# Gate logits of a mixture of experts: x as the stationary operand, and seven operations in a round of the normalisation in place of eight

## The chip, the cores and the metric

The kernel runs on one core of a Trainium2 chip. The metric is the device time of one execution in microseconds. The core's engines are named as in the profile: PE (TensorE, matmuls; PEld is its weight load), DVE (VectorE), ACT (ScalarE), POOL (GpSimd), SP (SyncE, which issues most DMAs).

## The reference

Attention in a window of 64, an ELU MLP on 2304 tokens of width 512, and then a mixture of 8 experts whose gates are normalised over rows and columns in turn. The change touches only how `logits` and `P` are computed.

```python
def _moe2_ref(x, w_gate, w1, w2):
    N, D = x.shape                      # 2304, 512
    E = w_gate.shape[1]                 # 8
    logits = x @ w_gate
    logits = logits - logits.max()
    P = np.exp(logits)
    for _ in range(8):
        P /= P.sum(1, keepdims=True) + 1e-09
        P /= P.sum(0, keepdims=True) + 1e-09
        P *= N / E
    out = np.zeros((N, D), dtype=np.float32)
    for e in range(E):
        h = np.maximum(x @ w1[e], 0.0)
        ye = h @ w2[e]
        out += P[:, e:e + 1] * ye
    return out
```

## The kernel before

The 2304 tokens lie in five blocks j of 512, 512, 512, 512 and 256 tokens. Every operand of a large matmul is split into a high part rounded to fp32r and a low part (the rest), and a product takes three fp32r matmuls. x of block j is held as `Xh[j]` and `Xl[j]`, features on the partitions, tokens along the free dimension, four chunks c of 128 features.

The order on every engine is that in which the code is written. The MLP runs in steps (u, j, i): u is one of four groups of 512 hidden features, i one of its four chunks. A step issues `step_in` (12 matmuls into a bank `p1`, then the ELU on ACT and DVE), and then `step_out` of the step two before it: 12 matmuls into four banks `ac` that stay open over i. At i = 3 DVE adds the four banks to `acc` (L493, `accs_done`), which frees them; there are four such banks, so `step_out` at i = 0 of the next block waits for these adds. The experts' stage follows in the same way: steps e0, e1, ... with `e_in` (12 matmuls, then `relu`: ACT writes `hh`, DVE writes `hl`) and `e_out` of two steps before (12 matmuls into four banks for the 512 tokens of block 0, 6 into two banks for the 256 tokens of block 1 that this stage takes). e0 and e1 are the two chunks of block 0 for the first unit of weights, e2 and e3 the same of block 1, and e4 opens the second unit, whose first `e_out` stands in e6; the `e_out` in e4 is that of e2 and opens block 1's two banks. When a unit's last chunk of a block is done, the banks are copied or added to `acc` (`e_done`: on ACT, L897, for the first unit).

Beside these steps a list `extra` is worked off. In the last group u = 3, when a block has its x complete, `moe1_out` appends for it: store x and split chunks 0 and 1, split chunks 2 and 3, nothing, `gate_a`, `gate_b`. One entry is taken at the end of a step of the MLP, up to two at the end of an experts' step while gates are left, and a step ends at a `gate_a`. `x2_split` makes the high part on ACT (L497) and leaves the low part on DVE (L501) to the next step. `gate_a` computes the logits of the block with the gate weights `gw` as the stationary operand (16 of its 128 columns are in use: the 8 high and the 8 low parts) and x as the moving one, 512 columns at a time; the result has 16 partitions. DVE copies it to `lgT`, and `gate_b` turns it with `sel`, a 16x8 matrix that also adds the two parts, so that a token comes to lie on a partition; the 8 logits of each token are copied to `Lg`. Behind the last block stand the entries of the normalisation (`sink_parts`): the maximum, the exponential, and eight rounds `rows` and `cols`, one entry a round.

When no gate is left in `extra`, the pool `big1` (x of blocks 2 to 4, `gw`) is closed and the pool B, which overlays it, is opened (`done2`). This lets through the tasks that prepare the experts' weights, `p_tasks`: for half an expert n, POOL makes four sums into `sw` (two buffers, L704), ACT writes the high parts of `rw` and `sw` (L729), DVE the low parts (L734), SP stores them. The tasks are let through by a table `due` against `clock`, the sum of 256-token units that the steps have done, and before `done2` only up to the 58th.

Of the kernel before, what the change touches and what calls it, by code (L numbers as in the profile page):

```python
# [8 lines left out]
F32 = mybir.dt.float32  # L9
# [3 lines left out]
ALU = mybir.AluOpType  # L13
AX = mybir.AxisListType
# [4 lines left out]
def kernel(  # L19
# [14 lines left out]
    nc = tc.nc  # L34
    B, H, S, D = q.shape
    NT, DM = out.shape
    DFF = w_in.shape[1]
    E, _, FF = w1.shape
    P = 128
    WIN = 64  # L40
    NCC = DM // P
# [5 lines left out]
    TB = 512  # L47
    scale = 1.0 / float(D) ** 0.5
    blocks = [(t, min(TB, NT - t)) for t in range(0, NT, TB)]
    NTT = NT // P  # L50

    def r(ap):
        return ap.bitcast(F32)

    const = ctx.enter_context(tc.tile_pool(name="const", bufs=1))
    def pool(name, side="left", **kw):
        cm = tc.tile_pool(name=name, bufs=1, side=side, reuse_waits="tile", **kw)
        return cm, cm.__enter__()
# [3 lines left out]


    mask = const.tile([P, P], F32, name="mask")
    sel = const.tile([2 * E, E], F32, name="sel")
    gwr = const.tile([P, NCC, E], F32, name="gwr")
    pad_cm, pad = pool("pad", side="right")
    ctx.callback(close, pad_cm)
# [4 lines left out]
    work_cm, work = pool("work")  # L73
# [9 lines left out]
    ident = const.tile([P, P], F32, name="ident")  # L83
    ones = const.tile([P, P], F32, name="ones")
    Lg = const.tile([P, NTT, E], F32, name="Lg")
# [3 lines left out]
    Xh = [home[j].tile([P, NCC, n], R32, name=f"xh{j}") for j, (_, n) in enumerate(blocks)]  # L89
    Xl = [home[j].tile([P, NCC, n], R32, name=f"xl{j}") for j, (_, n) in enumerate(blocks)]  # L90
# [12 lines left out]
    gw = big1.tile([P, NCC, P], R32, name="gw")  # L103
# [7 lines left out]
    def ps_sm(name):  # L111
        return ps.tile([P, 512], F32, tag="sm", bufs=1, name=name)
# [428 lines left out]
    def moe1_out(st, extra):  # L541
        step_out(st)
        u, j, i = st
        if u == NU - 1 and i == UF - 1:
            fs = [
                lambda: (x2_store(j), x2_split(j, (0, 1))), lambda: x2_split(j, (2, 3)),
                lambda: None, lambda: gate_a(j), lambda: gate_b(j),
            ]
            logits.append(fs[3])
            gate_fs.extend(fs)  # L550
            extra += fs
            if j == len(blocks) - 1:
                extra += sink_parts()


    lgT = {}

    def gate_a(j):
        n = blocks[j][1]
        lg = ps_sm("lg")  # L560
        for c in range(NCC):
            nc.tensor.matmul(lg[:, :n], gw[:, c, :], Xh[j][:, c, :], start=(c == 0), stop=False)
            nc.tensor.matmul(
                lg[:, :n], gw[:, c, :], Xl[j][:, c, :], start=False, stop=(c == NCC - 1)
            )
        t = work.tile([P, TB], F32, tag="m", bufs=2, name="lgT")[:2 * E]
        nc.vector.tensor_copy(t[:, :n], lg[:2 * E, :n])
        lgT[j] = t

    def gate_b(j):  # L570
        t0, n = blocks[j]
        lt = ps_sm("lt")
        nt = n // P
        t = lgT.pop(j)
        for tt in range(nt):
            nc.tensor.matmul(
                lt[:, tt * E:(tt + 1) * E], t[:, tt * P:(tt + 1) * P], sel, start=True, stop=True
            )
        nc.vector.tensor_copy(
            Lg[:, t0 // P:t0 // P + nt, :], lt[:, :nt * E].rearrange("p (t e) -> p t e", e=E)  # L580
        )

    sk = {}
# [1 line left out]
    def sink_parts():  # L585
        def small(shape, nm):
            return const.tile(shape, F32, name=nm)

        def p0():
            mx = small([P, 1], "mx")  # L590
            nc.vector.tensor_reduce(mx, Lg, axis=AX.XY, op=ALU.max)
            sk["mx"] = mx

        def p1():
            t = ps_sm("mxT")
            nc.tensor.matmul(t[0:1, :P], sk["mx"], ident, start=True, stop=True)
            nb = small([1, 1], "nb")
            nc.vector.tensor_reduce(nb, t[0:1, :P], axis=AX.X, op=ALU.max, negate=True)
            sk["nb"] = nb

        def p2():
            t = ps_sm("nbB")
            nc.tensor.matmul(t[:, 0:1], ones[0:1, :], sk["nb"], start=True, stop=True)
            nm = small([P, 1], "nm")
            nc.vector.tensor_copy(nm, t[:, 0:1])
            nc.scalar.activation(Pr, Lg, AF.Exp, bias=nm)
            sk["rs"] = small([P, NTT], "rs")
            sk["cs"] = small([P, E], "cs")
            sk["rc"] = small([P, E], "rc")

        def rows():
            rs, cs = sk["rs"], sk["cs"]
            nc.vector.tensor_reduce(rs, Pr, axis=AX.X, op=ALU.add)
            nc.vector.tensor_scalar(rs, rs, 1e-9, None, op0=ALU.add)
            nc.vector.reciprocal(rs, rs)
            nc.vector.tensor_tensor(
                out=Pr, in0=Pr, in1=rs.unsqueeze(2).to_broadcast([P, NTT, E]), op=ALU.mult
            )
            nc.vector.tensor_reduce(cs, Pr.rearrange("p t e -> p e t"), axis=AX.X, op=ALU.add)

        def cols():
            t = ps_sm("csum")
            nc.tensor.matmul(t[:, :E], ones, sk["cs"], start=True, stop=True)
            rc = sk["rc"]
            nc.vector.tensor_scalar(rc, t[:, :E], 1e-9, None, op0=ALU.add)
            nc.vector.reciprocal(rc, rc)
            nc.vector.tensor_scalar(rc, rc, float(NT) / E, None, op0=ALU.mult)
            nc.vector.tensor_tensor(
                out=Pr, in0=Pr, in1=rc.unsqueeze(1).to_broadcast([P, NTT, E]), op=ALU.mult
            )  # L630

        def first():
            p2()
            rows()

        def mid():
            cols()
            rows()

        return [p0, p1, first] + [mid] * 7 + [cols]  # L640
# [267 lines left out]
    def x2_store(j):  # L908
        if j == 1:
            for o, a in ((0, acc[j]), (2, acc1b)):  # L910
                nc.sync.dma_start(out=x2d[j][:, o:o + 2], in_=a.rearrange("p (c t) -> p c t", c=2))
        else:
            nc.sync.dma_start(out=x2d[j], in_=acc[j].rearrange("p (c t) -> p c t", c=NCC))
# [240 lines left out]
    with tc.manual_schedule():  # L1154
# [6 lines left out]
            out=mask[:WIN], in_=mask[:WIN], compare_op=ALU.is_gt, fill=-1.0e9 / scale,  # L1161
# [4 lines left out]
            out=mask[:WIN], in_=mask[:WIN], compare_op=ALU.is_ge, fill=-1.0e9 / scale,  # L1166
# [51 lines left out]
        for m in range(NST + 3):  # L1218
# [57 lines left out]
        nc.gpsimd.tensor_tensor(  # L1276
            out=gw[:, :, E:2 * E], in0=gwr, in1=r(gw[:, :, 0:E]), op=ALU.subtract
        )
        nc.vector.tensor_copy(sel[0:E, :], ident[0:E, 0:E])
        nc.sync.dma_start(out=sel[E:2 * E, :], in_=ident[0:E, 0:E])  # L1280
        run_bg(len(bg))
        bg += [w_tasks(2 * UF + m)[1] for m in range(2)]
        for kk in range(2 * UF + 2, 4 * UF):
# [20 lines left out]
        for s, st in enumerate(steps):  # L1304
            u, j, i = st
# [9 lines left out]
            while len(queue) > 2:  # L1315
                moe1_out(queue.pop(0), extra)
# [39 lines left out]
        for u in range(1, 2 * KP):  # L1356
            n = 5 if 0 <= u - 2 < len(others) - N1 - N3 else 4
# [5 lines left out]
        for s, st in enumerate(esteps):  # L1363
            _, u, j, x = st
# [57 lines left out]
        for s in range(NPD * 7 + LAG):  # L1422
            k, j = divmod(s, 7)
# [61 lines left out]
```

## Time and profile before

| | |
|---|---|
| median of three runs | 2016.78 us (2015.24 to 2019.64) |
| the profiled execution | 2017.01 us, span 2015.0 us |
| PE busy | 1990.0 us, 99% of the span |
| DVE busy | 1410.5 us, 70% |
| ACT busy | 871.4 us, 43% |
| POOL busy | 754.3 us, 37% |
| DMA queue q1 | 479.24 MB, 74.1% of 16 engines |

The span is what the profiler saw of the program; the execution's own time is some 2 us longer. Busy means that an instruction of the engine was under way; matmuls are pipelined, so that a new one starts before the last has ended.

### The profile page before, as it was taken

The page shows a single profiled execution, that of the slowest core. Times are in us where ns is not written, and L with a number is a line of the kernel's source. Part 1 is how long each engine was busy: PE and PEld are TensorE (multiplying, and loading weights), DVE is VectorE, ACT ScalarE, POOL GpSimd, SP SyncE. Part 2 cuts the span into 40 slices and gives each one's busy share as a digit, 9 for nine tenths or more (in the row PEclk, how much of TensorE's full clock was granted, in tenths as well). Part 3 has the DMA queues.
Part 4 walks back from the last instruction along what each step waited for, and adds up shares of the span by engine and source line. Part 5 has one row for each costly group of instructions (what it writes and reads, how often), then busy time and mean ns, then how long its engine had stood idle before and what let it go on. Part 6 is the DMA issues. An engine that isn't in the chain of part 4 may idle for free.

```text
span 2015.0 us, 36376 instructions
## 1 busy us (share of the span) xinstructions
PE 1990.0 (99%) x13190; PEld 1845.5 (92%) x13190; DVE 1410.5 (70%) x2727; ACT 871.4 (43%) x1839; POOL 754.3 (37%) x725
## 2 busy tenths in 40 slices
PE   9999999999999999999999999999999999999998
PEld 7778888888878888889999999999999999999998
DVE  6745676757688666557777777777777777777776
ACT  8866455545444343333343333333334333333332
POOL 5423242323355555343253233333334323333332
PEclk9999999999999999999999999999999999999999
DMA  9741254438599999958878777777888878777774
GB/s 210 161 106 40 79 177 153 164 126 317 203 368 339 368 367 357 343 192 275 278 247 276 248 247 249 250 250 250 250 278 263 257 250 250 250 248 249 248 248 129
DMA packets 290866, 481.59 MB, mean 239 GB/s; under 512 B 78528, under 2 KB 145152, under 8 KB 286848
## 3 DMA queue, kind: packets, MB, share of 16 engines
q1 hardware_dynamic: 290608, 479.24, 74.1%
q8 instruction: 105, 1.72, 0.3%
q14 instruction: 73, 0.60, 0.1%
q10 hardware_dynamic: 80, 0.03, 0.0%
HBM read 348.14 MB, written 126.88 MB: 236 GB/s over the span
## 4 chain that ended last, share of the span: by engine, by line
PE 86%; DVE 5%; issue 3%; DMA 2%; ACT 2%; POOL 1%; SPq 1%; DVEq 0%; POOLq 0%; ACTq 0%
PE la L1051 15%; PE ob L1124 13%; PE oa L1124 13%; PE lb L1051 11%; PE ac L883 2%; PE ac L884 2%; PE ac L885 2%; PE p L865 2%; PE p L866 2%; PE p L867 2%; PE p L204 2%; PE p L205 2%; PE p L206 2%; PE ac L532 2%; PE ac L533 2%
## 5 line engine op out<-in xcount | busy, mean ns | idle before, releaser
L1033 POOL TENSOR_TENSOR h<-s,h 128x384 fp32r<-128x384 f32 x304 | 373.0, 1246 | 712.9 <-ACT h L1024 641.8
L1051 PE MATMUL la<-xf,w1f 128*128 128x384 f32 x1824 | 361.4, 336 | 6.9 <-ACT a L1064 4.8
L1051 PEld LDWEIGHTS la<-xf,w1f 128*128 128x128 f32 x1824 | 311.7, 189 | 9.1 <-ACT a L1064 5.2
L1124 PE MATMUL oa<-w2f,h 128*128 128x256 f32 x2394 | 307.3, 282 | 0.8 <-DVE acc L1145 0.8
L1124 PE MATMUL ob<-w2f,h 128*128 128x256 f32 x2394 | 307.2, 282 | 0.0
L1124 PEld LDWEIGHTS oa<-w2f,h 128*128 128x128 f32 x2394 | 302.0, 190 | 1.0 <-DVE acc L1145 1.0
L1124 PEld LDWEIGHTS ob<-w2f,h 128*128 128x128 f32 x2394 | 302.0, 190 | 0.0
L1029 DVE SCALAR_TENSOR_TENSOR h<-c,h 128x384 fp32r<-128x384 f32 x228 | 211.0, 925 | 120.9 <-ACT h L1024 120.7
L1051 PE MATMUL lb<-xf,w1f 128*128 128x384 f32 x1368 | 274.8, 335 | 0.0
L1051 PEld LDWEIGHTS lb<-xf,w1f 128*128 128x128 f32 x1368 | 237.7, 189 | 0.2 <-DVE c L1081 0.2
L1024 ACT ACTIVATE h<-s 128x384 fp32r<-128x384 f32 x304 | 154.8, 524 | 146.9 <-DVE s L1068 60.8
L1024 ACT ACTIVATE h<-c 128x384 fp32r<-128x384 f32 x228 | 119.2, 523 | 183.1 <-DVE c L1059 125.9
L1145 DVE SCALAR_TENSOR_TENSOR acc<-oa,Pr,acc 128x256 f32<-128x256 f32 x393 | 165.2, 474 | 42.2 <-PE oa L1124 42.2
L1145 DVE SCALAR_TENSOR_TENSOR acc<-ob,Pr,acc 128x256 f32<-128x256 f32 x381 | 160.2, 474 | 40.4 <-PE ob L1124 40.4
L704 POOL TENSOR_TENSOR sw<-rw 128x256 f32<-128x256 f32 x110 | 103.8, 944 | 215.3 <-DVE f L734 161.1
L1064 ACT ACTIVATE v<-la 128x384 f32<-128x384 f32 x76 | 37.4, 492 | 199.7 <-PE la L1051 199.7
L246 ACT ACTIVATE hh<-p 128x512 fp32r<-128x512 f32 (+1 forms) x80 | 39.3, 491 | 193.7 <-PE p L867 193.7
L865 PE MATMUL p<-xh,f 128*128 128x512 f32 (+1 forms) x320 | 108.6, 340 | 0.0
L866 PE MATMUL p<-xl,f 128*128 128x512 f32 (+1 forms) x320 | 107.6, 336 | 0.0
L867 PE MATMUL p<-xh,f 128*128 128x512 f32 (+1 forms) x320 | 107.5, 336 | 0.0
L1068 DVE SCALAR_TENSOR_TENSOR s<-c,s 128x384 f32<-128x384 f32 x152 | 102.7, 676 | 5.4
L247 DVE SCALAR_TENSOR_TENSOR hl<-p,hh 128x512 fp32r<-128x512 f32 (+1 forms) x80 | 44.3, 555 | 88.8 <-ACT hh L246 88.7
(159 smaller groups left out, 3648.2 us busy)
## 6 DMA issues: line engine op xcount, KB each, us to landing
w1f<-wdi SPq DMA_DIRECT2D x532, 256.0 KB, 3.8
w2f<-wdo SPq DMA_DIRECT2D x266, 512.0 KB, 4.0
wdo<-f SPq DMA_DIRECT2D x28, 1024.0 KB, 7.4
rw<-in_moe_w_dram SPq DMA_DIRECT2D x220, 128.0 KB, 4.3
wdi<-f SPq DMA_DIRECT2D x27, 1024.0 KB, 6.9
wdo<-f SPq DMA_DIRECT2D x28, 768.0 KB, 5.2
wdi<-f SPq DMA_DIRECT2D x27, 768.0 KB, 4.6
raw<-in_moe_w_in_dram SPq DMA_DIRECT2D x16, 512.0 KB, 4.5
```

The costliest lines, as they stand in the source:

```text
L247: nc.vector.scalar_tensor_tensor(gl[:, :n], p1[:, :n], 0.0, r(gh[:, :n]), op0=ALU.max, op1=ALU.subtract)
L704: nc.gpsimd.tensor_tensor(out=sw[:, o], in0=a, in1=b, op=op)
L865: nc.tensor.matmul(p1[:, :n], w[:, s, 0, cs], xh, start=(c == 0), stop=False)
L866: nc.tensor.matmul(p1[:, :n], w[:, s, 0, cs], xl, start=False, stop=False)
L867: nc.tensor.matmul(p1[:, :n], w[:, s, 1, cs], xh, start=False, stop=(c == NCC - 1))
L1024: nc.scalar.activation(h[:, 0], src, AF.Relu if relu else AF.Copy)
L1029: nc.vector.scalar_tensor_tensor(h[:, 1], src, 0.0, r(h[:, 0]), op0=ALU.max, op1=ALU.subtract)
L1033: nc.gpsimd.tensor_tensor(out=h[:, 1], in0=src, in1=r(h[:, 0]), op=ALU.subtract)
L1051: nc.tensor.matmul(o, w[:, a, c, :], x[:, b, c, :], start=first and c == 0 and z == 0, stop=last and c == 1 and z == 2, skip_group_check=True,
L1068: nc.vector.scalar_tensor_tensor(d[nm], d[a], 0.0, d[b], op0=ALU.max, op1=op)
L1124: nc.tensor.matmul(o[:, c * HB2:(c + 1) * HB2], hs[p][:, a, c * P:(c + 1) * P], w[:, p, b, :], start=fresh and c != 1 and p == 0 and z == ...
L1145: nc.vector.scalar_tensor_tensor(a, src, pe, a, op0=ALU.mult, op1=ALU.add)
```

## The change

`gate_a` and `gate_b` become one entry `gate`. For each of the block's tiles of 128 tokens, x (high and low, four chunks of features) is the stationary operand, 128x128, and 16 columns of `gw` are the moving one: eight matmuls a tile into the 16 columns of the tile in one bank, where a token is already on a partition. DVE adds the two groups of 8 with one reduction straight into `Lg`. `sel` and its copy and DMA go. In `cols`, the factor N/E goes into the operation that adds 1e-9, and the separate multiplication goes.

```diff
--- before.py
+++ after.py
@@ -62,7 +62,6 @@
 
 
     mask = const.tile([P, P], F32, name="mask")
-    sel = const.tile([2 * E, E], F32, name="sel")
     gwr = const.tile([P, NCC, E], F32, name="gwr")
     pad_cm, pad = pool("pad", side="right")
     ctx.callback(close, pad_cm)
@@ -544,7 +543,7 @@
         if u == NU - 1 and i == UF - 1:
             fs = [
                 lambda: (x2_store(j), x2_split(j, (0, 1))), lambda: x2_split(j, (2, 3)),
-                lambda: None, lambda: gate_a(j), lambda: gate_b(j),
+                lambda: None, lambda: gate(j),
             ]
             logits.append(fs[3])
             gate_fs.extend(fs)
@@ -553,31 +552,20 @@
                 extra += sink_parts()
 
 
-    lgT = {}
-
-    def gate_a(j):
-        n = blocks[j][1]
-        lg = ps_sm("lg")
-        for c in range(NCC):
-            nc.tensor.matmul(lg[:, :n], gw[:, c, :], Xh[j][:, c, :], start=(c == 0), stop=False)
-            nc.tensor.matmul(
-                lg[:, :n], gw[:, c, :], Xl[j][:, c, :], start=False, stop=(c == NCC - 1)
-            )
-        t = work.tile([P, TB], F32, tag="m", bufs=2, name="lgT")[:2 * E]
-        nc.vector.tensor_copy(t[:, :n], lg[:2 * E, :n])
-        lgT[j] = t
-
-    def gate_b(j):
+    def gate(j):
         t0, n = blocks[j]
+        nt = n // P
         lt = ps_sm("lt")
-        nt = n // P
-        t = lgT.pop(j)
         for tt in range(nt):
-            nc.tensor.matmul(
-                lt[:, tt * E:(tt + 1) * E], t[:, tt * P:(tt + 1) * P], sel, start=True, stop=True
-            )
-        nc.vector.tensor_copy(
-            Lg[:, t0 // P:t0 // P + nt, :], lt[:, :nt * E].rearrange("p (t e) -> p t e", e=E)
+            for c in range(NCC):
+                for z, x in enumerate((Xh, Xl)):
+                    nc.tensor.matmul(
+                        lt[:, tt * 2 * E:(tt + 1) * 2 * E], x[j][:, c, tt * P:(tt + 1) * P],
+                        gw[:, c, 0:2 * E], start=(c == 0 and z == 0), stop=(c == NCC - 1 and z == 1),
+                    )
+        nc.vector.tensor_reduce(
+            Lg[:, t0 // P:t0 // P + nt, :],
+            lt[:, :nt * 2 * E].rearrange("p (t z e) -> p t e z", z=2, e=E), axis=AX.X, op=ALU.add,
         )
 
     sk = {}
@@ -622,9 +610,10 @@
             t = ps_sm("csum")
             nc.tensor.matmul(t[:, :E], ones, sk["cs"], start=True, stop=True)
             rc = sk["rc"]
-            nc.vector.tensor_scalar(rc, t[:, :E], 1e-9, None, op0=ALU.add)
+            nc.vector.tensor_scalar(
+                rc, t[:, :E], 1e-9, float(E) / NT, op0=ALU.add, op1=ALU.mult
+            )
             nc.vector.reciprocal(rc, rc)
-            nc.vector.tensor_scalar(rc, rc, float(NT) / E, None, op0=ALU.mult)
             nc.vector.tensor_tensor(
                 out=Pr, in0=Pr, in1=rc.unsqueeze(1).to_broadcast([P, NTT, E]), op=ALU.mult
             )
@@ -1276,8 +1265,6 @@
         nc.gpsimd.tensor_tensor(
             out=gw[:, :, E:2 * E], in0=gwr, in1=r(gw[:, :, 0:E]), op=ALU.subtract
         )
-        nc.vector.tensor_copy(sel[0:E, :], ident[0:E, 0:E])
-        nc.sync.dma_start(out=sel[E:2 * E, :], in_=ident[0:E, 0:E])
         run_bg(len(bg))
         bg += [w_tasks(2 * UF + m)[1] for m in range(2)]
         for kk in range(2 * UF + 2, 4 * UF):
```

What the list `extra` holds for a block is one entry shorter, and all that stands behind it in the list moves. Three places follow; the names are those of the tiles, numbers at their ends being buffers.

PE at the end of step (3, 2, 0), the gate of block 0, before (`lg` and `lt` are the two results in PSUM; the last three rows stand one step later):

```order
L533 MATMUL ac<-gh,w1l 128x512
L562 MATMUL lg<-xh_93,gw 128x512
L563 MATMUL lg<-xl_98,gw 128x512
...
L563 MATMUL lg<-xl_98,gw 128x512
L204 MATMUL p_5360<-xh_95,w0h 128x512
...
L533 MATMUL ac<-gh,w1l 128x512
L576 MATMUL lt<-sel,lgT 128x8 x4
L204 MATMUL p_5411<-xh_95,w0h 128x512
```

and with the change:

```order
L532 MATMUL ac<-gh,w1l 128x512
L562 MATMUL lt<-gw,xh_92 128x16
L562 MATMUL lt<-gw,xl_97 128x16
...
L562 MATMUL lt<-gw,xl_97 128x16
L203 MATMUL p_5380<-xh_94,w0h 128x512
L204 MATMUL p_5380<-xl_99,w0h 128x512
```

The eight matmuls with 512 moving columns and the later turn with `sel` are replaced by 32 matmuls with 16 moving columns, at the place where the first stood.

DVE in steps (3, 4, 0) and (3, 4, 1), before (`f` are the low parts of the experts' weights, `m` and `gl` belong to the ELU, `xl` is the low part of x, `acc` x4 are the adds that free the four banks of block 3):

```order
L501 TENSOR_TENSOR xl_100<-acc_104,xh_95 128x512 x2
L227 SCALAR_TENSOR_TENSOR m<-m,p_5725 128x256
L235 TENSOR_TENSOR gl<-m,gh 128x256
L734 TENSOR_TENSOR f_5712<-sw,f_5712 128x4x256
L493 TENSOR_TENSOR acc_105<-ac,acc_105 128x512 x4
L501 TENSOR_TENSOR xl_100<-acc_104,xh_95 128x512 x2
```

and with the change:

```order
L723 TENSOR_TENSOR f_5752<-rw,f_5752 128x4x256
L226 SCALAR_TENSOR_TENSOR m<-m,p_5762 128x256
L234 TENSOR_TENSOR gl<-m,gh 128x256
L723 TENSOR_TENSOR f_5752<-sw,f_5752 128x4x256
L566 TENSOR_REDUCE Lg<-lt 128x32
L492 TENSOR_TENSOR acc_104<-ac,acc_104 128x512 x4
L226 SCALAR_TENSOR_TENSOR m<-m,p_5836 128x256
L234 TENSOR_TENSOR gl<-m,gh 128x256
L500 TENSOR_TENSOR xl_100<-acc_104,xh_95 128x512 x2
```

The two `xl` rows of block 2 that stood ahead of the adds, between them and the `f` row, are gone from here (they stand a step earlier), and the reduction of block 2's gate stands just ahead of the adds.

ACT in steps e2 and e3, before (`hh` is the high part of the experts' hidden values, the `acc` x4 are the copies that free the four banks of e1's block):

```order
L246 ACTIVATE hh<-p_5977 128x256
L497 ACTIVATE xh_97<-acc_106 128x256 x2
L729 ACTIVATE f_6025<-rw 128x4x256
L729 ACTIVATE f_6025<-sw 128x4x256
L729 ACTIVATE f_6042<-rw 128x4x256
L729 ACTIVATE f_6042<-sw 128x4x256
L246 ACTIVATE hh<-p_6059 128x256
L897 ACTIVATE acc_103<-ac 128x512 x4
L497 ACTIVATE xh_97<-acc_106 128x256 x2
```

and with the change:

```order
L245 ACTIVATE hh<-p_6057 128x256
L718 ACTIVATE f_6116<-rw 128x4x256
L718 ACTIVATE f_6116<-sw 128x4x256
L718 ACTIVATE f_6133<-rw 128x4x256
L718 ACTIVATE f_6133<-sw 128x4x256
L718 ACTIVATE f_6150<-rw 128x4x256
L718 ACTIVATE f_6150<-sw 128x4x256
L245 ACTIVATE hh<-p_6167 128x256
L886 ACTIVATE acc_102<-ac 128x512 x4
L718 ACTIVATE f_6202<-rw 128x4x256
```

The last gate now falls in e2 instead of e4, so `done2` comes three steps sooner, and two more rows of the weights' preparation, `f_6150` from `rw` and from `sw`, stand ahead of the `hh` row and the four copies.

## Rows read from the trace of the kernel before

**Rows 1.** the page's first part: busy time, share of the span, instructions

```profile
PE 1990.0 (99%) x13190; PEld 1845.5 (92%) x13190; DVE 1410.5 (70%) x2727; ACT 871.4 (43%) x1839; POOL 754.3 (37%) x725
```

**Rows 2.** stretches: length, busy time (instructions) of each engine, granted clock, DMA share, GB/s

```profile
518.00:522.00 4.00, 4.00 (x14) 3.23 (x14) 3.22 (x6) 1.11 (x3) 1.15 (x2) 0.57 0.70 289
...
610.00:612.00 2.00, 0.91 (x5) 0.41 (x3) 1.83 (x6) 0.89 (x2) 1.26 (x2) 1.00 0.90 280
```

**Rows 3.** waits of PE: us in total, times, longest

```profile
PE ac L531 <- DVE acc L493: 2.3, 1, 2.3
...
PE csum L623 <- DVE cs L619: 2.1, 2, 1.5
...
PE ac L883 <- DVE acc L899: 1.1, 1, 1.1
```

**Rows 4.** PE in order of time, gate of block 0 (start, us)

```profile
460.55 0.39 PE L562 MATMUL lg<-xh,gw 128*128 128x512 f32 x1
...
462.36 0.39 PE L204 MATMUL p<-xh,w0h 128*128 128x512 f32 x1
...
467.57 0.39 PE L533 MATMUL ac<-gh,w1l 128*128 128x512 f32 x1
...
467.89 1.05 PE L576 MATMUL lt<-sel,lgT 16*128 16x8 f32 x8
...
469.21 0.40 PE L205 MATMUL p<-xl,w0h 128*128 128x512 f32 x1
```

**Rows 5.** weight loads in order of time, gate and experts

```profile
467.89 0.96 PEld L576 LDWEIGHTS lt<-sel,lgT 16*128 16x128 f32 x8 [0.35 <-issue]
...
701.71 0.19 PEld L865 LDWEIGHTS p<-xh,f 128*128 128x128 f32 x1
...
701.83 0.19 PEld L866 LDWEIGHTS p<-xl,f 128*128 128x128 f32 x1
```

**Rows 6.** PE in order of time, two long waits

```profile
514.34 0.28 PE L206 MATMUL p<-xh,w0l 128*128 128x256 f32 x1
...
516.90 0.35 PE L531 MATMUL ac<-gh,w1h 128*128 128x256 f32 x1 [2.28 <-DVE acc L493]
...
518.60 0.58 PE L531 MATMUL ac<-gh,w1h 128*128 128x256 f32 x1
...
522.43 0.28 PE L204 MATMUL p<-xh,w0h 128*128 128x256 f32 x1
...
893.90 2.21 PE L1051 MATMUL la<-xf,w1f 128*128 128x384 f32 x6 [4.84 <-ACT a L1064]
```

**Rows 7.** DVE in order of time, the first of these

```profile
510.79 2.37 DVE L501 TENSOR_TENSOR xl<-acc,xh 128x512 fp32r<-128x512 f32 x2
...
514.93 1.23 DVE L734 TENSOR_TENSOR f<-sw,f 128x1024 fp32r<-128x1024 f32 x1 [0.18 <-ACT f L729]
...
516.07 2.48 DVE L493 TENSOR_TENSOR acc<-ac,acc 128x512 f32<-128x512 f32 x4
```

**Rows 8.** DVE, POOL and ACT in order of time, steps e2 to e4

```profile
543.98 1.22 DVE L734 TENSOR_TENSOR f<-sw,f 128x1024 fp32r<-128x1024 f32 x1
...
545.28 1.65 POOL L704 TENSOR_TENSOR sw<-rw 128x256 f32<-128x256 f32 x1 [26.12 <-DVE f L734]
...
549.46 0.92 POOL L704 TENSOR_TENSOR sw<-rw,sw 128x256 f32<-128x256 f32 x1
...
542.07 1.05 ACT L729 ACTIVATE f<-sw 128x1024 fp32r<-128x1024 f32 x1
...
543.75 0.39 ACT L246 ACTIVATE hh<-p 128x256 fp32r<-128x256 f32 x1 [0.63 <-PE p L867]
...
544.39 2.65 ACT L897 ACTIVATE acc<-ac 128x512 f32<-128x512 f32 x4 [0.25 <-PE ac L885]
```

**Rows 9.** lines of the normalisation: times, ns least/median/most, first and last start

```profile
L627 DVE TENSOR_SCALAR rc<-rc x8: 171/344/714, 578.3 to 621.6; 128x8 f32<-128x8 f32 x8
...
L613 DVE TENSOR_REDUCE rs<-Pr x8: 303/303/306, 573.4 to 616.8; 128x18 f32<-128x144 f32 x8
```

## The prediction, on record before the run

> **What bounds the kernel now.** I read first the page's busy shares: PE is under way 99% of the span, DVE 70% [rows 1]. So what PE spends on an instruction is paid in full, and what another engine spends counts only where PE stands still for it. The list of PE's waits is short, and four of its places lie near the code that changes: banks of the MLP not yet added (2.3 us), the column sums of the normalisation (2.1 us in two places, the longest 1.5), a bank of the experts' stage (1.1 us) [rows 3]; the fourth is the clock. The stretches show PE's granted clock at 1.00 (2.4 GHz) all but everywhere, yet at 0.57 over 518 to 522, that is mostly at 1.2 GHz, after a wait [rows 2]. Then I read PE in order of time at a gate, for what the old matmuls take [rows 4, 5], and the three other engines at the two places where the new order puts something else ahead of what PE waits for [rows 6 to 8].
>
> **The matmuls of the gates.** Before, eight matmuls with 512 columns start at 460.55 and the next one behind them at 462.36: 1.81 us, 0.226 each [rows 4]. The turn with `sel` costs more than its share of work: the matmul before it starts at 467.57 and would have been followed at 467.80; L205 stands at 469.21, so its predecessor counts from 468.98: 1.18 us [rows 4]. That is 2.99 us a block, 12.0 for four, and I put the fifth, with half the tokens, at half, 1.5: 13.5 us go.
>
> Instead come 18 tiles x 8 = 144 matmuls, each with a full 128x128 stationary operand of its own and only 16 columns to move. The nearest row for the price is the turn itself: eight weight loads of 128 columns with 8 moving columns take 0.96 us, the last one its 0.187 alone, so (0.96 - 0.187) / 7 = 0.110 us each [rows 5]; there the weights had 16 rows, not 128. The other bound has 128 rows of the same type: loads of 0.19 us start 0.12 apart (701.71, 701.83) under matmuls of 256 columns, which set that pace themselves [rows 5]. So 0.110 to 0.120; I take 0.115: 16.6 us. Behind each gate the next large matmul waits for its own load, as L204 did behind the turn: from 468.87, its load's start, some 0.11 more than 0.226, five times, 0.5 us. Sum 17.1 us, 3.6 more than before (2.9 to 4.3).
>
> The Trainium skill, "TensorE: Matmul & The Clock Gate", section "Back-to-back issue gap", gives some 60 cycles for a matmul of up to 64 columns. An estimate by that page is 144 x 25 ns = 3.6 us, ten less than before; the trace's 0.110 us for 8 columns speaks against it, and I follow the row.
>
> **The first wait.** In before PE starts the last of 12 short matmuls at 514.34 and then waits 2.28 us until 516.90 [rows 6]. It waits for DVE's adds at 516.07. DVE was late because the two `xl` of block 2 (2.37 us from 510.79), two ELU rows and an `f` row stood ahead [rows 7]. In what follows the clock is low: the three matmuls of 256 and eight of 512 columns from 518.60 to 522.43 take 3.83 us in place of 3 x 0.12 + 1.81 = 2.17 [rows 6], so the fall itself costs 1.7 us. All of it: from 514.46 to 522.43, 7.97 us for 12 x 0.12 + 1.81 = 3.25 us of work, 4.7 us lost. With the change `xl` stands a step earlier, and PE reaches the four banks a gate (32 x 0.115 = 3.7 us) later, while the `f` row ahead of the adds comes up to 2.4 us sooner. Both put DVE there before the banks: -4.7 us. Late next would be the reduction of gate 2 ahead of the adds, but its matmuls end 12 x 0.12 + 0.7 us before the first bank.
>
> **The wait that comes instead.** The last gate falls in e2, and `done2` lets the sixth weight row on ACT, the high part of `sw` of the next half expert, stand ahead of `hh` of e3 and of the four copies that free banks. Its POOL sums need a `sw` buffer that DVE's second `f` row frees, and that row now stands behind the reduction of the last gate, hence behind PE. From the end of that gate: PE's results and the reduction some 0.4 (0.3 for a reduction of this kind [rows 9]); two `f` rows of 1.22 [rows 8]; POOL's four sums as in before from 545.28 to 549.46 + 0.92, 5.1; ACT's row 1.05, `hh` 0.39, the first copy 2.65 / 4 = 0.66 [rows 8]. Sum 10.0 us. PE in that time does e3 (12 x 0.12 + 12 x 0.226 = 4.2) and `e_in` of e4 (2.7), 6.9 us, and stands before the bank for 3.0 us; its matmuls behind that bank, and through them all else, wait. In before the gates were not yet done here and the copies followed PE at once (0.25 us at 544.39). The fall of the clock comes with it, as after the waits of 2.28 and 4.84 us (six matmuls in 2.21 us after the latter [rows 6]); the wait of 1.5 us in 610 to 612 left it at 1.00 [rows 2, 3]. So +3.0 and +1.7.
>
> **The normalisation.** One DVE operation of 171 to 714 ns, 344 at the median, leaves seven of its eight rounds' hand-overs and the last round [rows 9], some 2.8 us of DVE in all, which count only where PE waits for a sum. The rounds start two steps sooner, when DVE has had PE's new wait to catch up, and no pair of `f` rows stands ahead of the last column sum any more. I take 2.7 us off the 3.2 us of waits in this stage [rows 3]; the bounds are 0 and 3.2.
>
> `sel`'s copy and DMA, DVE's copies of `lg` and `lt` and the earlier stores of x on SP cost and gain nothing: PE's weights and DVE's rows there have a step's slack or more, and SP's next loads wait for the same last block as before.
>
> **Sum:** 3.6 - 4.7 + 3.0 + 1.7 - 2.7 = +0.9 us. The profiled execution took 2017.01 us, 0.2 above the median of the runs shown; so 2017.9 us.
>
> **Rivals.** Less than 0.2% (4.0 us) is about what a measurement of this kernel can tell from no change.
>
> *The clock falls in the gates.* For 3.7 us PE does little but load weights, and 144 x 16 columns are what 4.5 matmuls of 512 have. No row shows what such a stretch does to the clock; the turn with `sel` was too short (1 us). Were it taken as a wait, it would be longer than the 2.28 us that sufficed. At 1.7 us a fall, two to four falls give 2021.3 to 2024.7: slower from two on. The Trainium skill, same page, section "A second HAM failure mode: psum-queue depth-cycling", says that short idle times between groups of matmuls alone make the clock swing. By that page this rival would hold; in 610 to 612 a short wait did not do it. Chance 0.28.
>
> *The wait in e4 stays away*, if POOL or ACT run sooner than in before or the clock holds: up to -4.7, 2013.2, with the loads at 0.110 2012.5. For it speaks that POOL's first two sums took 1.65 us and its last 0.92; against it that DVE is just as busy there. Chance 0.16.
>
> *The waits of the normalisation stay*: +2.7, 2020.6. Chance 0.09.
>
> *Small matmuls without the price of their loads*: ten us less, 2008. Chance 0.03.
>
> *Loads that don't overlap*: 144 x 0.19 = 27.4 us, 14 more than before in place of 3.6, 2028. Against it the loads 0.12 apart [rows 5]. Chance 0.05.
>
> **How the numbers follow.** The forecast has 0.39. Faster by over 0.2%: 0.03 of the small matmuls, 0.09 of the wait that stays away and 0.02 of others, 0.14. Slower: 0.23 of the clock, 0.05 of the loads, 0.04 of the rest, 0.32. Within 0.2%: 0.54. The range from 2012.0 to 2023.5 leaves out the loads, the small matmuls and the end of the clock's rival, some 0.18. The forecast's own is 2015.5 to 2020.
>
> **What would show it.** 144 matmuls of 16 columns at 0.110 to 0.120 us, a granted clock of 1.00 in the gates, no wait for L492 at the adds of block 3, a wait of PE in e4 for L886's copies of about 3 us with a low clock behind it, and no wait of over 0.5 us for a column sum. Wrong makes it a low clock in the gates above all, then the wait in e4 of another size.

## The result and the profile after

The change makes the kernel slower: 2036.70 us, the median of five runs (2034.28 to 2043.54), against 2017.18 us for the kernel before, ratio 1.0103 with a 95% interval of 1.009 to 1.0116 (the two medians alone give 1.0097). The prediction was 2017.9 us, its range ended at 2023.5. A sixth execution of the changed kernel took 9657 us for a reason that the records don't show; it is left out of the median, of the ratio and of all that follows. The profiled execution took 2036.39 us, its span is 2034.6 us.

The page of the changed kernel shows the same picture as [rows 1], with 21 us more of PE:

```profile
PE 2011.4 (99%) x13258; PEld 1863.1 (92%) x13258; DVE 1402.7 (69%) x2713; ACT 870.7 (43%) x1839; POOL 759.4 (37%) x725
```

PE's waits from 200 to 880 us (us in total, times, longest), which answer to [rows 3]:

```profile
PE ac L872 <- ACT acc L886: 3.1, 1, 3.1
PE lt L562 <- ACT xh L496: 2.0, 1, 2.0
PE p L484 <- DVE gl L234: 1.1, 2, 0.7
PE lt L562 <- DVE xl L500: 1.1, 1, 1.1
```

The banks of the MLP (2.3 us) and the column sums (2.1 us) are gone, as forecast; the copies in e4 cost 3.1 us, as forecast (3.0), and by the path that was forecast: POOL's sums wait for DVE's `f` row, ACT's row waits for the sums, and PE for the copies behind it.

```profile
558.58 1.65 POOL L693 TENSOR_TENSOR sw<-rw 128x256 f32<-128x256 f32 x1 [27.83 <-DVE f L723]
564.29 1.06 ACT L718 ACTIVATE f<-sw 128x1024 fp32r<-128x1024 f32 x1 [7.71 <-POOL sw L693]
566.16 0.79 PE L872 MATMUL ac<-f,hh 128*128 128x512 f32 x1 [3.12 <-ACT acc L886]
```

Not forecast are the two waits of `lt` L562, which are in gate 2. In all PE waits for 7.3 us here, and for 7.4 us in the same stretch of before: the waits moved, but their sum is not what makes the kernel slower.

PE in order of time at gate 0, to be held against [rows 4]:

```profile
462.11 0.17 PE L562 MATMUL lt<-gw,xh 128*128 128x16 f32 x1
462.14 0.26 PE L562 MATMUL lt<-gw,xl 128*128 128x16 f32 x1
...
465.49 0.26 PE L562 MATMUL lt<-gw,xl 128*128 128x16 f32 x1
465.60 0.49 PE L203 MATMUL p<-xh,w0h 128*128 128x512 f32 x1
465.93 0.40 PE L204 MATMUL p<-xl,w0h 128*128 128x512 f32 x1
466.16 0.40 PE L205 MATMUL p<-xh,w0l 128*128 128x512 f32 x1
...
467.42 0.63 PE L203 MATMUL p<-xh,w0h 128*128 128x512 f32 x1
467.85 0.63 PE L204 MATMUL p<-xl,w0h 128*128 128x512 f32 x1
```

Thirty distances from 462.14 to 465.49 make 0.112 us a matmul, and PE is never idle. But 1.8 us behind the gate the large matmuls, which started 0.23 apart, start 0.43 apart. The stretches (columns as in [rows 2]; the third number from the end is the granted clock) show why:

```profile
460.00:466.00 6.00, 6.00 (x45) 5.56 (x44) 4.52 (x6) 4.13 (x6) 0.56 (x2) 1.00 0.79 287
466.00:470.00 4.00, 4.00 (x13) 3.09 (x12) 1.09 (x2) 0.00 (x0) 3.67 (x4) 0.59 1.04 380
490.00:494.00 4.00, 4.00 (x31) 3.77 (x31) 2.10 (x3) 2.64 (x3) 1.00 (x2) 1.00 0.95 325
494.00:498.00 4.00, 4.00 (x13) 3.09 (x12) 0.06 (x1) 0.99 (x2) 1.84 (x3) 0.57 0.84 347
...
518.00:528.00 10.00, 9.24 (x41) 9.05 (x42) 7.86 (x11) 5.90 (x10) 5.08 (x5) 0.50 0.77 273
...
545.00:549.00 4.00, 4.00 (x15) 3.30 (x13) 0.00 (x0) 0.54 (x1) 0.00 (x0) 0.57 0.00 0
...
566.00:569.00 3.00, 2.84 (x6) 1.82 (x6) 1.83 (x4) 3.00 (x7) 2.73 (x3) 0.50 1.10 379
```

The clock falls to 1.2 GHz behind gates 0, 1 and 3, where PE has waited for nothing, for some 10 us in gate 2 and the step behind it, and behind the wait in e4. Taken together that is some 24 us at half speed, which do the work of 12, where before had, from 200 to 880 us too, one such stretch of less than 4 us [rows 2]: some 10 us lost. It is not the profiled execution alone: the mean granted clock of the five timed executions is 0.990 to 0.994, and 0.995 to 0.999 in the executions of the kernel before that were timed beside the experiments below; 0.005 of 2036 us is again some 10 us.

The wait in gate 2 begins on ACT and SP. Their rows in order of time (start, length; SP's rows issue DMAs), and then the two rows of ACT in before that answer to them:

```profile
507.33 0.63 ACT L230 ACTIVATE gh<-m 128x512 fp32r<-128x512 f32 x1 [2.24 <-DVE m L226]
515.78 1.06 ACT L718 ACTIVATE f<-rw 128x1024 fp32r<-128x1024 f32 x1 [7.82 <-DMA wdo<-f]
516.75 1.13 ACT L496 ACTIVATE xh<-acc 128x512 fp32r<-128x512 f32 x2
```
```profile
503.96 2.38 SPq L679 DMA_DIRECT2D rw<-in_moe_w_dram  x4
506.39 0.47 SPq L902 DMA_DIRECT2D x2d<-acc  x1
506.90 0.44 SPq L728 DMA_DIRECT2D wdo<-f  x1
507.44 1.01 SPq L729 DMA_DIRECT2D wdo<-f  x1
```
```profile
503.85 1.06 ACT L729 ACTIVATE f<-rw 128x1024 fp32r<-128x1024 f32 x1 [5.55 <-DMA wdo<-f]
...
509.33 1.13 ACT L497 ACTIVATE xh<-acc 128x512 fp32r<-128x512 f32 x2
```

The second pair of `xh` of block 2 stands behind ACT's `f<-rw`, which waits until the store of an earlier `f` from the same memory has landed. That store stands on SP behind four loads, which had waited for a DVE `f` row for 10.6 us, and the store of x, and leaves at 506.90. In before the same ACT row waited too (5.5 us, until 503.85), but `xh` of block 2 was not behind it, since it stood one entry later in the list. PE is in gate 2 at 514.87 and finds half of x not split.

Waits, matmuls and clock do not cover it all. ACT's `v`, which is written 76 times in the last stage, runs from 896.9 to 2005.0 after, 1108.1 us, and from 881.8 to 1985.4 before, 1103.6 us. Nothing of the change is in that stage.

### The profile page after: what moved, and what is told of

Read it like the earlier page. It is cut to its first block, busy times and chain, and to the rows that moved or that the text cites. A ratio compares the mean times of both kernels' runs of the same rounds, so it can differ in the third digit from the quotient of the medians.

```text
span 2034.6 us, 36490 instructions
## 1 busy us (share of the span) xinstructions
PE 2011.4 (99%) x13258; PEld 1863.1 (92%) x13258; DVE 1402.7 (69%) x2713; ACT 870.7 (43%) x1839; POOL 759.4 (37%) x725
## 4 chain that ended last, share of the span: by engine, by line
PE 91%; DVE 3%; issue 2%; DMA 2%; ACT 1%; SPq 0%; POOL 0%; DVEq 0%; ACTq 0%; POOLq 0%
PE la L1040 15%; PE ob L1113 13%; PE oa L1113 13%; PE lb L1040 11%; PE ac L872 3%; PE ac L874 3%; PE ac L873 3%; PE p L854 3%; PE p L855 3%; PE p L856 3%; PE p L205 2%; PE p L204 2%; PE p L203 2%; PE ac L530 2%; PE ac L531 2%; PE ac L532 2%
```

## The experiments

Each was timed against the kernel before in the same job, whose median there was 2017.8 to 2019.4 us; kernels of different jobs are compared below by their ratios. **Old places** means that a block's list has a fifth, empty entry, so that all that comes later stands where it stood before; **new places** the four entries of the change; **wide** that all 128 columns of `gw` move; **narrow** the 16 of the change; **room** that the 32 bytes of `sel` stay free.

| kernel | gates | places | addresses | median us | ratio (95%) |
|---|---|---|---|---|---|
| norm_only | as before | old | as before | 2016.36 | 0.9984 (0.9973 to 0.9996) |
| turn_new_places | as before | new | as before | 2023.00 | 1.0020 (1.0009 to 1.0031) |
| the change | narrow | new | 32 lower | 2036.70 | 1.0103 (1.009 to 1.0116) |
| narrow_old_places | narrow | old | 32 lower | 2035.52 | 1.0083 (1.0066 to 1.0100) |
| wide_new_places | wide | new | 32 lower | 2035.24 | 1.0077 (1.0060 to 1.0093) |
| after_room | narrow | new | as before | 2027.59 | 1.0046 (1.0030 to 1.0061) |
| before_32_lower | as before | old | 32 lower | 2029.13 | 1.0047 (1.0032 to 1.0062) |
| narrow_old_room | narrow | old | as before | 2028.35 | 1.0044 (1.0032 to 1.0056) |
| wide_old_room | wide | old | as before | 2022.67 | 1.0020 (1.0009 to 1.0030) |
| wide_ahead_room | wide | new, reordered | as before | 2023.36 | 1.0019 (1.0010 to 1.0029) |
| narrow_ahead_room | narrow | new, reordered | as before | 2025.17 | 1.0039 (1.0027 to 1.0050) |
| norm_64_lower | as before | old | 64 lower | 2020.12 | 1.0013 (1.0004 to 1.0021) |
| norm_96_lower | as before | old | 96 lower | 2023.94 | 1.0032 (1.0021 to 1.0043) |
| norm_ahead | as before | old, reordered | as before | 2019.73 | 1.0004 (0.9995 to 1.0012) |
| after_room_end | narrow | new | constants 32 lower | 2029.61 | 1.0049 (1.0034 to 1.0063) |

All but before_32_lower have the shorter normalisation.

### Form, places and normalisation apart

*norm_only*: the kernel before with the second hunk of the normalisation alone. 

> The kernel before with one operation less in each round of the normalisation and nothing else. Both theories: the waits for the column sums (2.1 us) shrink by up to as much: 2015 to 2017.5. If all of the 3.2 us of waits in that stage go with the operation: 2014.

 Measured 0.9984; the waits for column sums are gone from PE's list, all of them. This is also the only version here that is faster than the kernel before.

*turn_new_places*: the old matmuls in the new places.

```diff
-                lambda: None, lambda: gate_a(j), lambda: gate_b(j),
+                lambda: None, lambda: gate_a(j),
...
         lgT[j] = t
+        later.append(lambda: later.append(lambda: gate_b(j)))
```

> The kernel before, its gates with 512 columns and the turn with sel, but in a list of four entries as in the change (the turn is put a step later by the queue of late work), and with the shorter normalisation. Theory 1: the clock holds in the gates; what the shifted places cost by themselves is the wait for the high parts of x in gate 2 (about 3 us and a fall, 1.7) and the wait in e4 (3 and 1.7), less the first wait (4.7) and the normalisation's (3): 2018 to 2022. Theory 2: 2030 to 2036.

 Measured 1.0020, 2023.00 us, 1 us above the range of theory 1, and 0.36% or 7.3 us above norm_only. PE's waits from 500 to 870 us:

```profile
PE lt L577 <- DVE lgT L567: 3.8, 1, 3.8
PE ac L885 <- ACT acc L899: 3.1, 1, 3.1
PE lg L563 <- DVE xl L501: 0.8, 1, 0.8
PE lg L562 <- ACT xh L497: 0.3, 1, 0.3
```

The banks of the MLP don't stop PE any more, but gate 2 stops it for `xh`, `xl` and then the turn, and e4 for its 3.1 us, without a single narrow matmul. The longest wait, 3.8 us, is the turn's; the change has no turn, so this run is not the price of the places in the change.

*narrow_old_places*: `lambda: None, lambda: gate(j), lambda: None,` in the list. 

> The changed kernel with a fifth, empty entry behind each gate in a block's list, so that all later pieces (splits of x, gates, weight rows, last gate) stand a step apart as in the kernel before; matmuls and normalisation are those of the change. Theory 1 (the narrow matmuls, which do little but load weights, bring TensorE's clock down in the gates): gates at 0.11 us a matmul still cost 3.6 us more, four of them leave the clock at 1.2 GHz for some 3.5 us, which costs 1.7 us each; with the wait at 514 to 522 as before and the normalisation's 3 us gone: 2024 to 2029. Theory 2 (the shifted places cost it all): the waits for the high parts of x in gate 2 and for the copies in e4 go, the clock holds but for the fall of before, 2017 to 2020.

 Measured 2035.52 us, beyond both theories: the waits of gate 2 and of the copies in e4 are gone, the wait for the banks of block 3 is back (2.3 us), with a low clock from 524.4 to 538.1 us, and 6 us or more came from neither theory.

*wide_new_places*:

```diff
-                        lt[:, tt * 2 * E:(tt + 1) * 2 * E], x[j][:, c, tt * P:(tt + 1) * P],
-                        gw[:, c, 0:2 * E], ...
+                        lt[:, tt * P:(tt + 1) * P], x[j][:, c, tt * P:(tt + 1) * P],
+                        gw[:, c, :], ...
```

> The changed kernel with all 128 columns of gw moving (112 of them zero) in place of 16, so the same 144 weight loads with eight times the columns. Theory 1: the pitch stays near 0.11 us, set by the loads, and the clock holds at 2.4 GHz in the gates, which saves four falls of 1.7 us and the long low stretch behind gate 2's wait in part: 2024 to 2030. Theory 2: as the change, 2036 to 2041. If columns don't matter to the clock and only the loads do: as the change too, with a low clock in the gates.

 No clock falls in gates 0, 1, 3 and 4 any more, as theory 1 says, but the time is 5 us above its range. So the first theories did not hold the whole of it. What the kernels over 2030 us share is that `sel` is missing and the last stage is longer: 1108.7 us from first to last `v` in narrow_old_places and 1108.4 in wide_new_places, but 1104.4 in norm_only and 1103.7 in turn_new_places, which have `sel`. `sel` takes 32 bytes of each partition, near the bottom of the left side; without it all tiles above on that side lie 32 bytes lower.

### The 32 bytes

*after_room*: the change with an unused tile in the place of `sel`.

```diff
+    room = const.tile([P, E], F32, name="room")
     gwr = const.tile([P, NCC, E], F32, name="gwr")
```

> The changed kernel with an unused tile of 32 bytes a partition where sel stood, so that every tile behind it lies at its address of before; nothing else differs. Theory A (addresses: without sel all tiles of the left side lie 32 bytes lower, and the matmuls that read them take longer, 228.6 in place of 227.2 ns in the first MLP steps and 119.85 in place of 119.4 ns in the last stage): the pitches of before come back, the last stage falls from 1147 to 1143 us, in all 7 to 10 us less than the change: 2028 to 2032. Theory B (the longer last stage comes from the gates' form or from the run): as the change, 2036 to 2041, pitches as there.

 Measured 1.0046, 0.57% less than the change, 11.5 us. (The 119.4 and 119.85 ns that these expectations name are those of the `oa` matmuls. The traces of before and of before_32_lower give 119.36 and 119.95 ns over the distances that lie within 3% of their median, and 119.28 and 119.57 ns over all; for `la` it is 175.1 and 176.3 ns over all.)

*before_32_lower*: the reverse, with the very instructions of before.

```diff
-    sel = const.tile([2 * E, E], F32, name="sel")
+    sel = mask[0:2 * E, 0:E]
```

> The kernel before with sel put into a corner of the mask, which is no longer read by then: every tile behind it lies 32 bytes lower, at its address in the change; no instruction is added or taken away. Theory A: 7 to 10 us more than before, 2025 to 2029, with 119.85 ns a matmul in the last stage. Theory B: as before, 2015 to 2020.

 Measured 1.0047, 9.5 us. ACT's `v` in the last stage (times, ns least/median/most, first and last start), first of before, then of before_32_lower, the change and after_room:

```profile
L1064 ACT ACTIVATE v<-la x76: 474/492/493, 881.8 to 1985.4; 128x384 f32<-128x384 f32 x76
```
```profile
L1064 ACT ACTIVATE v<-la x76: 473/492/492, 887.8 to 1995.8; 128x384 f32<-128x384 f32 x76
```
```profile
L1053 ACT ACTIVATE v<-la x76: 472/492/492, 896.9 to 2005.0; 128x384 f32<-128x384 f32 x76
```
```profile
L1054 ACT ACTIVATE v<-la x76: 475/492/493, 891.4 to 1996.3; 128x384 f32<-128x384 f32 x76
```

1103.6, 1108.0, 1108.1 and 1104.9 us: the stage follows the addresses and not the gates. The MLP's steps show it too. From the first `step_in` of these groups to the first matmul of gate 0, where there is not yet any difference of order, it is 248.8 us before (211.7 to 460.5) and 248.9 in after_room (211.9 to 460.8), but 250.7 in before_32_lower (213.4 to 464.1) and in the change (211.4 to 462.1). No wait on PE's list accounts for it, and neither does the clock: the mean granted clock of the timed executions is 0.997 in before and in before_32_lower. The distances between matmuls grow: in the last stage by some 0.3 ns over 4522 recorded distances of `oa` and `ob`, and by 1.1 to 1.3 ns over 2703 of `la` and `lb`. That makes some 4.7 us, enough for the 4.4.

*narrow_old_room* and *wide_old_room*: room together with old places. 

> The changed kernel with the fifth, empty entry in each block's list and with the 32 bytes of sel kept free. Theory A: 7 to 10 us less than with the empty entry alone, 2025 to 2030; what is left over the kernel before is the matmuls' 3.6 us and low clock at the gates, less the normalisation's 3. Theory B: 2033 to 2038, as without the room.

 

> As narrow_old_room, with all 128 columns of gw moving. Theory A: addresses of before, and the clock holds in the gates, so that only the 3.6 us of the matmuls less the normalisation's 3 remain: 2016 to 2022. Theory B: 2028 to 2034.

 Measured 1.0044 and 1.0020. The room gives back 7.9 us (0.39%) against narrow_old_places. The two differ by 0.24%, 4.9 us, with the same weight loads, the same places and addresses. From 460 to 590 us the clock is low for 30.7 us in the narrow kernel and for 13.6 in the wide one, which is 8.5 us at half speed; the wide one waits some 3.6 us longer. So the clock makes the difference, and covers a longer wait besides. wide_old_room is a little above its range; PE waits 3.5 us there for the banks of block 3, and the granted clock is 0.51 from 518 to 525 and 0.50 from 525 to 531.6 us, with gate 2 in the midst.

*after_room_end*: the 32 bytes free behind the last constant. 

> The changed kernel with 32 unused bytes behind the last of the constants: gwr, ident, ones, the gate values and the other constants lie 32 bytes lower as in the change, the big tiles (x, weights, forms, accumulators) at their addresses of before. If the big tiles that TensorE reads decide: as after_room, 2025 to 2031, with 119.4 ns in the last stage. If the constants decide: as the change, 2036 to 2041, with 119.85 ns.

 Measured 1.0049: as after_room. So it is the big tiles, not the constants.

*norm_64_lower* and *norm_96_lower*: norm_only with `sel` and `mx`, then `nm` too, put into the mask. 

> The kernel before with the shorter normalisation, and with sel and mx put into the mask, so that the big tiles of the left side lie 64 bytes lower. If the place within 64 bytes decides: 119.4 ns a matmul in the last stage and the time of norm_only, 2012 to 2018. If any shift costs, or the place within 128 bytes decides: 119.6 to 119.9 ns and 2021 to 2028.

 

> The same with nm in the mask too, 96 bytes lower. If the place within 64 bytes decides: 119.85 ns in the last stage, 7 to 10 us above norm_64_lower. If the place within 128 bytes decides, and 64 lower was slow: 119.4 ns.

 Measured 1.0013 and 1.0032 against 0.9984 for norm_only. Every shift tried costs, 5.8 and 9.7 us, and not by the place within 64 or 128 bytes alone. But it does not cost everywhere alike. The MLP's stretch that took 248.8 us in before takes 250.4 and 250.7 us with 64 and 96 bytes, as with 32. The last stage takes 1104.2 us with 64 bytes, as in norm_only, and 1105.9 with 96:

```profile
L1065 ACT ACTIVATE v<-la x76: 472/492/493, 886.4 to 1990.6; 128x384 f32<-128x384 f32 x76
```

With 64 bytes `oa` is as slow as with 32 (119.56 ns) and `la` faster than in before (174.9 ns against 175.1). Each kind of matmul has its own good and bad shifts; no rule was found.

### Both waits taken away by order

*wide_ahead_room* and *narrow_ahead_room* have the new places and two edits of order; the first puts the entry of `extra` ahead of the weights' rows in the MLP's steps.

```diff
+                if extra:
+                    extra.pop(0)()
-                elif su > 2:
+                if su > 2:
                     while ntask < min(5 * NPRE + 3, 3.4 * (su - 2)):
                         ptasks.pop(0)()
                         ntask += 1
-            if extra:
-                extra.pop(0)()
...
-            if s >= 2 and not done2 and ...
+            if s >= 5 and not done2 and ...
```

> The changed kernel (four entries in the list) with three things set right: the 32 bytes of sel kept free, 128 columns moving in the gates, and both new waits taken away by order alone: in the MLP steps the splits of x stand ahead of the weights' rows (so ahead of the row on ACT that waits for a store to land), and the sixth weight row stays where it was until e5. If places, addresses and clock are the whole of it: no wait at gate 2, none in e4, no low clock from 460 to 870; 3.6 us for the matmuls, less the first wait (4.7) and the normalisation (3): 3 to 5 us less than the kernel before, 2013 to 2016. Rival (the gates cost more than their 144 loads for a reason not seen yet): 2020 to 2025, with waits or low clock elsewhere.

 

> As wide_ahead_room, but with the 16 moving columns of the change. If the few columns bring the clock down: a low clock in at least three of the gates although PE never waits there, 1.7 to 3.4 us each, 5 to 12 us above wide_ahead_room. If only the waits did: the same time as wide_ahead_room, clock at 2.4 GHz.

 Measured 1.0019 and 1.0039. The wait of gate 2 shrank to 0.9 us and the one in e4 went, but others came. PE's waits in wide_ahead_room, 200 to 870 us:

```profile
PE ac L876 <- DVE acc L892: 2.5, 1, 2.5
PE csum L615 <- DVE cs L611: 2.2, 1, 2.2
PE p L485 <- DVE gl L235: 1.5, 2, 0.8
PE lt L563 <- DVE xl L501: 0.9, 2, 0.8
```

On DVE five `f` rows in a row (564.91 to 571.7 us) and a sixth at 574.16 now stand ahead of the adds at 575.88 and of the next sum: the weight rows that were held back come in a bunch. The time of the rival came, and its waits and low clock elsewhere, but not its reason: a gate takes 3.52 us here, no more than its 32 loads were put at. The pair shows the clock best. Stretches of wide_ahead_room at gates 0 and 3, and then of narrow_ahead_room at gate 0 and behind it, and at gate 1 and behind it:

```profile
463.90:467.50 3.60, 3.60 (x34) 3.60 (x33) 2.90 (x4) 2.62 (x5) 0.16 (x1) 1.00 0.11 33
...
535.60:539.20 3.60, 3.60 (x35) 3.60 (x34) 0.06 (x1) 0.00 (x0) 0.00 (x0) 1.00 0.00 0
```
```profile
459.80:463.40 3.60, 3.60 (x34) 3.60 (x33) 2.90 (x4) 2.61 (x5) 0.19 (x1) 1.00 0.09 29
464.00:467.40 3.40, 3.40 (x10) 2.67 (x9) 2.06 (x2) 0.00 (x0) 2.26 (x2) 0.51 0.99 357
486.80:490.40 3.60, 3.60 (x34) 3.59 (x33) 2.36 (x3) 2.29 (x4) 0.00 (x0) 1.00 0.94 335
491.40:494.80 3.40, 3.40 (x10) 2.63 (x9) 0.43 (x1) 0.43 (x1) 2.81 (x4) 0.50 1.03 424
```

As many matmuls in as long a gate, PE and its loads busy throughout in both. Behind the gates with 16 moving columns the clock falls; in the wide kernel no fall begins in or behind gates 0, 1, 3 and 4. In its gate 2, in which PE waits 0.9 us, the clock falls too (low from 516.3 to 523.1). The two kernels are 0.2% apart, 4 us, a little less than the expectation's 5 to 12. The number of falls varies between kernels with the narrow form. In or behind gates 0, 1 and 3, in which PE waits for nothing, the clock falls in 14 of 18 cases in the six narrow kernels (three of three in the change, one in narrow_old_places), and in none of nine in the three wide ones.

*norm_ahead*: norm_only with the first of those edits. 

> The kernel before with the shorter normalisation, and with the splits of x ahead of the weights' rows in the MLP steps; addresses and gates as before. If the first wait (at 514 to 522) hangs on the xl and f rows ahead of DVE's adds, as the prediction says: no wait for the adds and no low clock there, up to 4.7 us less than norm_only, 2011 to 2014. If the wait only moves to another row: within 2 us of norm_only, 2014 to 2018.

 Measured 1.0004, 4 us above norm_only: worse than both expectations. PE's wait for the adds grew from 1.9 to 5.0 us. DVE ahead of them:

```profile
515.82 2.38 DVE L501 TENSOR_TENSOR xl<-acc,xh 128x512 fp32r<-128x512 f32 x2
518.12 0.41 DVE L227 SCALAR_TENSOR_TENSOR m<-m,p 128x256 f32<-128x256 f32 x1
519.01 0.73 DVE L235 TENSOR_TENSOR gl<-m,gh 128x256 fp32r<-128x256 f32 x1 [0.48 <-ACT gh L231]
520.99 1.22 DVE L735 TENSOR_TENSOR f<-sw,f 128x1024 fp32r<-128x1024 f32 x1 [1.25 <-ACT f L730]
522.14 2.47 DVE L493 TENSOR_TENSOR acc<-ac,acc 128x512 f32<-128x512 f32 x4
```

`xl` still stands between the `f` rows and the adds, because it waits in the queue of late work; ACT's `gh` waits for DVE behind it, and now the next `xh` stands ahead of ACT's `f`. The edit did not take away what it aimed at: the wait grew by 3.1 us and the time by 4, and what stands ahead of the adds sets it.

## Why the prediction was wrong, step by step

The ratios add up, each with some 2 to 4 us either way by its intervals. From the kernel before to norm_only it is -3.2 us (-0.16%), from there to after_room, which has the new form of the gates and the new places, +12.5, and from there to the change +11.5 (the 32 bytes): +20.8 us, the measured 1.03%. The +12.5 does not split into form and places. With the old matmuls the new places cost 7.3 us (turn_new_places against norm_only, with the turn's own wait of 3.8 us), and the new form then 5.2. With the old places kept, the new form costs 12.1 us (narrow_old_room against norm_only), and the new places then 0.4 (after_room against narrow_old_room; without the room, the change against narrow_old_places, it is 4.0). Both kernels with the new form and the room have a mean granted clock of 0.991 to 0.992 over their timed executions, norm_only 0.997; 0.005 of 2027 us is some 10 us, so most of the +12.5 is clock. Against the terms of the sum:

- **"`sel`'s copy and DMA ... cost and gain nothing" failed, and it is the largest.** The instructions of `sel` cost nothing, but its memory did: without its 32 bytes, 9.5 us (on the kernel before) to 11.5 us (on the change) are lost in distances between matmuls nearly all over the program. The prediction weighed what instructions and queues do and never asked what a removed tile moves. Shown by after_room and before_32_lower, from both sides.
- **A granted clock of 1.00 in the gates failed; the rival of the clock, with a chance of 0.28, came true.** Behind gates 0, 1 and 3 of the change the clock falls without a wait. The price of a fall was right: 3.4 us at half speed are 1.7 us. The three pairs of kernels that differ only in the moving columns differ by 4.0, 4.9 and 5.2 us, and all the low clock of the change, behind waits too, makes some 10 us. No row of before could show it. The Trainium skill, "TensorE: Matmul & The Clock Gate", section "A second HAM failure mode: psum-queue depth-cycling", lays such a swing of the clock in another kernel to short idle times of PE between groups of matmuls. In gates 0, 1 and 3 the profile shows no idle time of PE, so the trace shows a fall without what that section names; the ends of matmuls are modelled in the profile, so idle time within the array is not excluded.
- **"the earlier stores of x on SP cost and gain nothing: PE's weights and DVE's rows there have a step's slack or more" failed.** The slack was looked for on PE and DVE, but ACT's `xh`, which moved with them, came to stand behind a row that waits for a store. The first wait did go from the banks, as the prediction said, but 3.1 us came back in gate 2, and the clock stayed low for 10 us there, through the rest of the gate and the step behind it. Places and waits were put at -4.7 + 3.0 + 1.7 = 0.0. That the new places cost only 0.4 to 4.0 us under the new form is luck, not a confirmation: what went at the banks came back in gate 2, which the sum did not have.
- **The gates' matmuls, +3.6: right, slightly high.** A gate of 32 takes 3.49 us from its first matmul to L203, and L204 starts 0.10 late; for 4.5 gates' worth and five ends 16.2 us against the 13.5 that went: +2.7, at full clock. The 0.112 us a matmul stand where the turn's row put them, as the prediction held. The Trainium skill, "TensorE: Matmul & The Clock Gate", section "Back-to-back issue gap", gives the 60 cycles that the prediction's 25 ns come from for a matmul by itself; in a stream in which each matmul has its weight load, it says, the load and the matmul set the spacing together. The trace agrees with the second and not with the first: 3.49 us a gate with 16 moving columns and 3.52 with 128.
- **The wait in e4, +3.0 and +1.7: right.** 3.1 us, and 3.4 us of low clock behind it; from the matmul behind the last gate (555.75) to the first behind the wait (566.16) it is 10.4 us, where the sum had 10.0 from the end of the gate.
- **The normalisation, -2.7: right.** norm_only measures -3.2 us (-0.8 to -5.4).

What stays open: why the 32 bytes cost anything. `la` reads two tiles that did not move (both lie on the right side) and has slower matmuls nevertheless, and neither the place within 64 nor within 128 bytes orders the four addresses tried. No run here changed what else is read or written in the same memory at that time. Why the clock falls behind most narrow gates and not all is open too.

## What to carry to other kernels

A tile that goes is a change of every address behind it: when a small edit costs time in a stage that it doesn't touch, put the bytes back as an unused tile before looking further, and compare the distance between two instructions that no edit touched. When an entry of a list goes, follow every engine's rows that move up, and ask of each what stands ahead of it there and for which transfer that waits. The narrow gates kept PE busy throughout in the profile and still lost the clock, so a price per matmul at full clock is only a lower bound there. And when two edits are taken apart, take them apart in both orders: here the same places cost 7.3 us with one form and 0.4 with the other.

## What the runs showed that was not expected

- The same program with its left-side tiles 32 bytes lower is 0.47% slower (0.32 to 0.62%), 64 and 96 bytes lower some 0.3 and 0.5% against norm_only; with 64 bytes the last stage is as fast as with none.
- Gates of 32 matmuls of 128x128 loads last 3.5 us at full clock whether 16 or 128 columns move, and 6.7 us at half clock with either (gate 2 of narrow_old_places and of wide_old_room). Where PE does not wait in them, the clock falls in or behind most of the narrow ones and none of the wide ones. Once the clock is low, as behind the wait of 3.5 us in wide_old_room, even the wide gate leaves it low (518 to 531.6).
